# A feed-forward weight kept by halves: one quarter goes out to DRAM and back, one is converted in the double block

## The chip, the cores and the metric

One core of one Trainium2 chip runs the kernel. The metric is the device time of one execution in microseconds (us); several runs are given as their median. Engines are TensorE (PE; its weight loads are PEld), VectorE (DVE), ScalarE (ACT), GpSimd (POOL) and SyncE (SP), whose queue issues nearly all transfers.

## The reference

Three layers follow each other, in float32; the inputs w_in and w_out arrive as 8-byte floats, which the kernel reads as pairs of int32 and converts itself.

```python
def reference(**kwargs):
    attn_out = _attn_ref(**attn_kwargs)      # 4 x 8 heads, 576 positions, 64 columns; causal, with a decay from cumsum(s)
    x = np.ascontiguousarray(attn_out.transpose(0, 2, 1, 3)).reshape(B * S, H * D)   # 2304 x 512
    x = _moe_ref(x=x, **moe_kwargs)          # soft mixture: d.T @ x gives 32 slots, 8 experts of 4 slots, c @ slot_out
    return _moe2_ref(x=x, **moe2_kwargs)     # h = x @ w_in; g = piecewise square of h; g @ w_out
```

In the mixture, slot_out has 32 rows of 512, c is 2304 x 32, and x = c @ slot_out. So h = x @ w_in = c @ (slot_out @ w_in): the product M = slot_out @ w_in, 32 x 2048, is made once, and the hidden products have only 32 rows to sum over (96 with the parts of a split float).

## The kernel before, in words

**Attention** (lines 166 to 672). 32 heads go in 16 pairs. A plan of times (PLAN, GATE, one pair is 12 units; `at` and `step` put an action at a time) is sorted and gives each engine's order. Among its actions are `next(pre)` from `load_parts` (line 116), which issues one load of an expert weight tile (128 x 1024 floats, 512 KB) into a free slot, and the steps W0 to W4, which advance `convert_wi` (line 606): a chunk of w_in is loaded (128 x 512 int32), GpSimd scales the high words (L626), VectorE shifts the low words (L627) and joins them (L629) into `wif`, which holds all of w_in, four quarters, unfinished. `finish_wi` (line 633) ends the conversion by four VectorE operations for each of 16 parts (L639 to L642); they run in the experts' stage.

**Experts** (lines 713 to 832). `layer1` and `layer2` take the eight experts in turn; W_ORDER is the order of the 64 weight tiles. 22 slots (16 named post, N_LEFT = 6 named pre) are filled in attention; when attention's memory is freed, 6 more pre slots (N_RIGHT) and 10 others (N_TMP) follow. `release` gives a layer's slots back and `load_w` issues the next loads, in one order on SP's queue. Tiles of w_out (wo) follow the experts' on that queue, six at a time at most, all but the first two behind a small `gate` transfer that waits for the last expert tile.

**Double block** (from line 834). A step is one (j, c): 384 tokens and 128 of the 2048 hidden columns; the first two blocks of tokens go side by side, so 16 columns take 32 steps. A step i of the loop at line 954 does: VectorE's g and ScalarE's gh of step i - 1 (`g_part`, L889, L891); TensorE's hidden product hp of step i and ScalarE's two w (`h_part`, L879, L881, L882); a part of the conversion of w_out, in five parts per tile (`convert_wo`: ScalarE's Prelu cv, VectorE's shift and join, ScalarE's cast wh, VectorE's rest wl; L154 to L158, L786, L788), one tile in two steps; VectorE's gl of step i - 1 (`l_part`, L897); and the nine output products of step i - 2 (`o_part`, L907 to L909).

hp reads 96 rows of `mst`: M twice rounded, and its rest. Before the loop, `m_part` makes the first 128 columns of all four quarters (16 products), `split_m` writes the first quarter's into mst (ScalarE twice, VectorE once; L858, L859), then come the other 384 columns (16 products), `split_m` again, and `stack_m` (L863 to L868), which rounds the other three quarters in m_hi and m_lo and carries their rows into mst by nine transfers.

The program adds semaphore waits itself. For two engines that touch one bank of PSUM it lets one wait for the other; each transfer waits for the one eight before it (eight counters, DMAHW0 to DMAHW7, in turn).

## Time and profile before

| | |
|---|---|
| runs, median of 3 | 460.08 us (459.59 to 461.58) |
| profiled execution, own time | 463.19 us |
| its span | 461.4 us |
| PE, DVE, ACT, POOL busy | 443.8, 326.7, 339.0, 45.3 us |
| moved by transfers | 71.02 MB |
| mean granted TensorE clock | 0.98 |

A busy time is the sum of an engine's instructions. TensorE counts as busy in 96% of the span whether or not its products come as closely as they could, so the table does not say what bounds a stage; the chain of waits and the starts of single instructions do. All times in the sections below are from the start of the span of the profiled execution.

### The profile page before, as it was taken

What the parts mean: (1) busy time and instruction counts of PE and PEld (TensorE: products, weight loads), DVE (VectorE), ACT (ScalarE), POOL (GpSimd) and SP (SyncE); (2) the same over time, 40 slices, a digit from 0 to 9 for tenths busy, and PEclk for the clock granted to TensorE, in tenths of its full rate; (3) what the DMA queues carried; (4) which work ended last, traced back from release to release, by engine and by line L of the source; (5) the groups of instructions that cost most, each with busy time, mean ns of one, the idle gap of its engine ahead of it and who ended that gap; (6) DMA issues with size and microseconds to landing.
All of it is one profiled execution on the core that took longest, in us unless ns stands there. A gap on an engine that the chain in (4) does not pass through costs nothing.

```text
span 461.4 us, 11656 instructions
## 1 busy us (share of the span) xinstructions
PE 443.8 (96%) x4306; PEld 336.8 (73%) x4306; DVE 326.7 (71%) x966; ACT 339.0 (73%) x914; POOL 45.3 (10%) x168
## 2 busy tenths in 40 slices
PE   7999999999999998898889999999999999999996
PEld 2676766776777676566546888888888888888885
DVE  6687899899988863699838888866555555455543
ACT  6998998998999894122248999977677767777673
POOL 2222212422222111000000000000000000000000
PEclk9799999999999998799999999999999999999999
DMA  3888879977897258699985900003001001001001
GB/s 86 228 219 217 255 218 294 265 225 192 221 279 237 67 170 287 216 390 407 409 294 196 362 2 1 0 2 136 1 0 68 1 1 70 1 0 56 14 1 68
DMA packets 28554, 71.02 MB, mean 154 GB/s; under 512 B 4018, under 2 KB 5490, under 8 KB 28498
## 3 DMA queue, kind: packets, MB, share of 16 engines
q1 hardware_dynamic: 28342, 70.14, 47.7%
q8 instruction: 34, 0.56, 0.5%
q14 instruction: 22, 0.18, 0.2%
q10 hardware_dynamic: 156, 0.14, 0.1%
HBM read 64.83 MB, written 4.83 MB: 151 GB/s over the span
## 4 chain that ended last, share of the span: by engine, by line
PE 83%; DVE 6%; DMA 5%; ACT 4%; issue 2%; POOL 0%; ACTq 0%; POOLq 0%; DVEq 0%; SPq 0%
PE o L909 14%; PE o L907 14%; PE o L908 14%; PE s L291 9%; PE s L399 7%; PE s L360 5%; DMA wt<-in_w_dram 4%; PE hp L879 4%; PE s L434 3%; PE p L736 2%; PE s L299 2%; PE s L391 2%; PE p L752 2%; ACT P L350 1%; DVE s L305 1%
## 5 line engine op out<-in xcount | busy, mean ns | idle before, releaser
L907 PE MATMUL o<-wt,gh 128*128 128x512 f32 x288 | 112.6, 391 | 0.6 <-ACT gh L891 0.6
L909 PE MATMUL o<-wt,gl 128*128 128x512 f32 x288 | 112.3, 390 | 0.2 <-DVE gl L897 0.2
L908 PE MATMUL o<-wt,gh 128*128 128x512 f32 x288 | 112.1, 389 | 0.0
L350 ACT ACTIVATE P<-s,nm 128x256 f32<-128x256 f32 (+4 forms) x160 | 85.0, 551 | 9.1 <-DVE nm L305 6.8
L897 DVE TENSOR_TENSOR gl<-g,gh 128x384 fp32r<-128x384 f32 x96 | 53.5, 557 | 42.1 <-ACT gh L891 42.0
L305 DVE CUSTOM_DVE_ANT_0 s<-s,tri 128x256 f32<-128x256 f32 (+4 forms) x160 | 74.0, 506 | 12.6 <-PE s L291 6.2
L891 ACT CAST gh<-g 128x384 fp32r<-128x384 f32 x96 | 49.3, 513 | 45.1 <-DVE g L889 42.6
L889 DVE SCALAR_TENSOR_TENSOR g<-w,hp 128x384 f32<-128x384 f32 x96 | 53.1, 553 | 37.2 <-ACT w L882 37.2
L907 PEld LDWEIGHTS o<-wt,gh 128*128 128x128 f32 x288 | 54.3, 188 | 12.8 <-ACT gh L891 1.1
L909 PEld LDWEIGHTS o<-wt,gl 128*128 128x128 f32 x288 | 54.0, 188 | 12.5 <-DVE gl L897 1.3
L908 PEld LDWEIGHTS o<-wt,gh 128*128 128x128 f32 x288 | 54.4, 189 | 7.5
L291 PE MATMUL s<-x 64*128 64x512 f32 (+3 forms) x256 | 57.1, 471 | 0.0
L881 ACT ACTIVATE w<-hp,half 128x384 f32<-128x384 f32 x96 | 55.4, 577 | 0.8 <-PE hp L879 0.8
L882 ACT ACTIVATE w<-w 128x384 f32<-128x384 f32 x96 | 50.4, 525 | 3.0
L383 ACT COPY pts<-s 128x512 f32<-128x512 f32 (+3 forms) x128 | 47.8, 463 | 1.5 <-PE s L360 0.5
L360 PEld LDWEIGHTS s<-ident,P 64*128 64x128 f32 x800 | 38.6, 142 | 10.9 <-ACT P L350 4.8
L360 PE MATMUL s<-ident,P 64*128 64x64 f32 x800 | 44.2, 229 | 2.3 <-ACT P L350 2.2
L399 PE MATMUL s<-pts,v 128*64 128x512 f32 (+3 forms) x256 | 38.9, 446 | 0.0
L350 ACT ACTIVATION_READ_ACCUMULATOR P<-s,nm 128x1 f32 x160 | 36.8, 230 | 0.0
L879 PE MATMUL hp<-cstack,mst 96*128 96x384 f32 x96 | 32.6, 343 | 0.3 <-DVE mst L859 0.3
L291 PEld LDWEIGHTS s<-x 64*128 64x128 f32 x256 | 29.3, 196 | 4.2 <-DMA x<-in_qkT_dram 1.5
L399 PEld LDWEIGHTS s<-pts,v 128*64 128x64 f32 x256 | 18.5, 141 | 17.5 <-issue 15.3
(149 smaller groups left out, 567.2 us busy)
## 6 DMA issues: line engine op xcount, KB each, us to landing
wt<-in_w_dram SPq DMA_DIRECT2D x64, 512.0 KB
x<-in_qkT_dram SPq DMA_DIRECT2D x32, 288.0 KB
st<-in_w_in_dram SPq DMA_DIRECT2D x32, 256.0 KB
wt<-in_w_out_dram SPq DMA_DIRECT2D x16, 512.0 KB
out_dram<-ob SPq DMA_DIRECT2D x17, 256.0 KB
v<-in_v_main_dram SPq DMA_DIRECT2D x16, 256.0 KB
ext<-exts SPq DMA_DIRECT2D x60, 3.4 KB
v<-in_v_tail_dram SPq DMA_DIRECT2D x16, 32.0 KB
```

Of the source, the lines that this page charges most:

```text
L291: T.matmul(out=o[h][:, off:off + n], lhsT=y[r, 0, c:c + 128], rhs=y[r, 1, 0:n], start=(k == 0), stop=(k == 1))
L305: V.tensor_tensor_reduce(out=sc, in0=sc, in1=mask[:, mask.shape[1] - n:], scale=-1.0 / SCALE, scalar=init, op0=ALU.add, op1=ALU.min, accum ...
L350: A.activation(out=out_, in_=in_, func=AF.Exp, bias=nm, scale=-1.0, accum_out=sm[:, k:k + 1])
L360: T.transpose(out=o[f][:, c:c + 64], in_=P[r], identity=ident[r, r])
L399: T.matmul(out=o[r, 128 * j:512], lhsT=vt[:, j, r], rhs=pts_t[pi][:, h, 512 * j:384 * j + 512], start=(j == 0), stop=(j == 3))
L879: T.matmul(out=hp, lhsT=mst[0:96, 128 * c:128 * c + 128], rhs=cstack[0:96, BLK * j:BLK * j + BLK], start=True, stop=True)
L881: A.activation(out=w, in_=hp, func=AF.Relu, bias=half, scale=0.5)
L889: V.scalar_tensor_tensor(out=g, in0=w, scalar=1.0, in1=hp, op0=ALU.min, op1=ALU.max)
L897: V.tensor_tensor(out=gl, in0=g, in1=gh.bitcast(F32), op=ALU.subtract)
L907: T.matmul(out=o_t[j][t], lhsT=gh[:, r], rhs=wh[c], start=(c == 0), stop=False)
L908: T.matmul(out=o_t[j][t], lhsT=gh[:, r], rhs=wl[c], start=False, stop=False)
L909: T.matmul(out=o_t[j][t], lhsT=gl[:, r], rhs=wh[c], start=False, stop=(c == 15))
```

## The change

w_in is no longer kept whole. `wif` has room for two quarters (WI_KEEP = 2), which takes 16 KB less on each partition, and N_LEFT goes from 6 to 10 slots of 4 KB. In attention, three quarters are converted. Quarter 2 (WI_AWAY) comes first: it is finished at once, by a third VectorE operation per chunk, and each chunk is stored to DRAM (w_in_f) by a transfer on SP's queue. Quarters 0 and 1 follow as before; `finish_wi` has 8 parts. The conversion's steps move to the pairs of W_PAIRS, and four early loads are added at four times near attention's end (PRE_AT).

Quarter 3 (WI_LATE) is loaded raw after the experts, by `load_wi`, called ahead of M: four tiles of it, then two of quarter 2 back from DRAM, all into pre slots. The loop converts quarter 3 by `convert` (the Prelu, shift and join of w_out) at the steps 5, 7, 8, 10, 11, 13, 14 and 16. M is made by quarters: 0 and 1 before the loop, 2 and 3 by 16 products each behind hp of the steps 10 and 18, in the 128 columns of the bank that hp leaves free. `split_m` writes quarter 0 in four parts, and `stack_m` carries a quarter's rows by 12 transfers of 32 x 128.

```diff
@@ -30,8 +30,12 @@
...
 N_HOME = 16
-N_LEFT = 6
+N_LEFT = 10
 N_RIGHT = 6
+WI_KEEP = 2
+WI_AWAY = (2,)
+WI_LATE = (3,)
+W_PAIRS = (1, 2, 3, 4, 6, 7, 8, 10, 11, 12, 14)
 N_TMP = (7, 3)
...
@@ -48,13 +52,15 @@
...
 CHUNK = 256
-WI_0 = (0,)
+WI_0 = (0, 3)
 WARM_T = (9, 4, 2, 3, 4)
-PRE_FROM, PRE_STEP = (5, 2.4)
+PRE_AT = [3 * int(5 + 2.4 * _n) + 0.76 for _n in range(22)] + [171.76, 177.76, 183.76, 186.76]
 NWIN = 2
...
 BLK = 384
+M_AT = {10: 2, 18: 3}
+LATE_AT = 5
...
@@ -101,10 +107,12 @@
...
-    wif = wip.tile([128, 4, 4, 512], F32, name="wif")
+    wif = wip.tile([128, WI_KEEP, 4, 512], F32, name="wif")
+    w_dram = ctx.enter_context(tc.tile_pool(name="w_dram", bufs=1, space=bass.MemoryType.DRAM))
+    w_in_f = {fb: w_dram.tile([128, 2048], F32, name=f"w_in_f{fb}") for fb in WI_AWAY}
     w_src = {"w1": w1, "w2": w2, "wo": w_out.bitcast(I32)}
-    w_tiles, w_wo, wo_used = {}, {}, []
+    w_tiles, w_wo, w_wi, wo_used = {}, {}, {}, []
     w_next = [0]
...
@@ -600,39 +608,57 @@
...
         pre = load_parts()
-        for n in range(N_HOME + N_LEFT):
-            at(3 * int(PRE_FROM + PRE_STEP * n) + 0.76, lambda: next(pre, None))
+        for t in PRE_AT:
+            at(t, lambda: next(pre, None))
+
+        n_fb = 2048 // CHUNK
+        wi_order = [(fb, k) for fb in (*WI_AWAY, *range(WI_KEEP)) for k in range(n_fb)]
...
-            n_all = 2048 * 4 // CHUNK
-            sts = {}
+            sts, spill = {}, []
             def get(n):
-                if n < n_all:
-                    fb, k = divmod(n, 2048 // CHUNK)
+                if n < len(wi_order):
+                    fb, k = wi_order[n]
                     sts[n] = stage.tile([128, 2 * CHUNK], I32, tag="st", name="st")
                     nc.sync.dma_start(out=sts[n], in_=w_in.bitcast(I32)[fb, :, 2 * CHUNK * k:2 * CHUNK * (k + 1)])
+
+            def put():
+                if spill:
+                    fb, k, d = spill.pop(0)
+                    nc.sync.dma_start(out=w_in_f[fb][:, CHUNK * k:CHUNK * (k + 1)], in_=d)
...
             yield
-            for n in range(n_all):
-                fb, k = divmod(n, 2048 // CHUNK)
+            for n, (fb, k) in enumerate(wi_order):
                 st = sts.pop(n)
-                d = wif[:, fb].rearrange("p c f -> p (c f)")[:, CHUNK * k:CHUNK * (k + 1)]
+                away = fb in WI_AWAY
+                d = wif[:, WI_KEEP - 1 if away else fb].rearrange("p c f -> p (c f)")[:, CHUNK * k:CHUNK * (k + 1)]
+                di = d.bitcast(I32)
                 w = st.rearrange("p (n two) -> p n two", two=2)
...
                 G.tensor_scalar(d, hi.bitcast(F32), 2.0 ** -112, 1.0, op0=ALU.mult, op1=ALU.mult)
-                V.tensor_scalar(lo, lo, 1, 0x70000000, op0=ALU.logical_shift_right, op1=ALU.bitwise_and)
+                if away:
+                    V.tensor_scalar(lo, lo, 29, None, op0=ALU.logical_shift_right)
+                    yield
+                    V.scalar_tensor_tensor(out=di, in0=di, scalar=3, in1=lo, op0=ALU.logical_shift_left, op1=ALU.bitwise_or)
+                    yield
+                    V.scalar_tensor_tensor(out=di, in0=hi, scalar=-0x80000000, in1=di, op0=ALU.bitwise_and, op1=ALU.bitwise_or)
+                else:
+                    V.tensor_scalar(lo, lo, 1, 0x70000000, op0=ALU.logical_shift_right, op1=ALU.bitwise_and)
+                    yield
+                    V.tensor_tensor(out=di, in0=di, in1=lo, op=ALU.bitwise_or)
+                get(n + 2)
+                put()
+                if away:
+                    spill.append((fb, k, d))
                 yield
-                V.tensor_tensor(out=d.bitcast(I32), in0=d.bitcast(I32), in1=lo, op=ALU.bitwise_or)
-                get(n + 2)
-                yield
...
-            for n in range(16):
+            for n in range(4 * WI_KEEP):
                 fb, k = divmod(n, 4)
...
@@ -660,7 +686,7 @@
...
                     step(n, f, pi)
-            for k in range(5) if pi else WI_0:
+            for k in (range(5) if pi in W_PAIRS else ()) if pi else WI_0:
                 step(f"W{k}", next, cw, None)
...
@@ -840,47 +866,81 @@
...
-    M_A = 128
-    mp = [ps_e.tile([128, 512], F32, tag="e", name="mp") for _ in range(2)]
-
-    def m_part(a, b, cs):
-        for c in cs:
-            for fb in range(4):
-                T.matmul(out=mp[a > 0][32 * fb:32 * fb + 32, a:b], lhsT=soT[:, c], rhs=wif[:, fb, c, a:b],
+    mp = [ps_e.tile([128, 128], F32, tag="e", name="mp") for _ in range(WI_KEEP)]
+    ps_w = []
+
+    def m_part(out, w):
+
+        for c in range(4):
+            for g in range(4):
+                T.matmul(out=out[32 * g:32 * g + 32, :], lhsT=soT[:, c], rhs=w(c)[:, 128 * g:128 * g + 128],
                          start=(c == 0), stop=(c == 3))
-    m_hi = fin[0].tile([128, 512], F32R, tag="m_hi", name="m_hi", bufs=1)
-    m_lo = fin[0].tile([128, 512], F32R, tag="m_lo", name="m_lo", bufs=1)
-    ps_w = []
-
-    def split_m(a, b):
+    def split_m(m, g):
+
+        q, c = slice(32 * g, 32 * g + 32), slice(128 * g, 128 * g + 128)
         for r in range(2):
-            A.copy(out=mst[32 * r:32 * r + 32, a:b], in_=mp[a > 0][0:32, a:b])
-        V.tensor_tensor(out=mst[64:96, a:b], in0=mp[a > 0][0:32, a:b], in1=mst[0:32, a:b].bitcast(F32), op=ALU.subtract)
-
-    def stack_m():
-        for r in (slice(0, M_A), slice(M_A, 512)):
-            A.copy(out=m_hi[:, r], in_=mp[r.start > 0][:, r])
-            V.tensor_tensor(out=m_lo[:, r], in0=mp[r.start > 0][:, r], in1=m_hi[:, r].bitcast(F32), op=ALU.subtract)
-        for fb in range(1, 4):
+            A.copy(out=mst[32 * r:32 * r + 32, c], in_=m[q])
+        V.tensor_tensor(out=mst[64:96, c], in0=m[q], in1=mst[0:32, c].bitcast(F32), op=ALU.subtract)
+
+    def stack_m(fb, m):
+
+        m_hi, m_lo = (fin[0].tile([128, 128], F32R, tag=n, name=n, bufs=2) for n in ("m_hi", "m_lo"))
+        A.copy(out=m_hi, in_=m)
+        V.tensor_tensor(out=m_lo, in0=m, in1=m_hi.bitcast(F32), op=ALU.subtract)
+        for g in range(4):
             for r in range(3):
-                nc.sync.dma_start(out=mst[32 * r:32 * r + 32, 512 * fb:512 * fb + 512].bitcast(F32),
-                                  in_=(m_hi if r < 2 else m_lo)[32 * fb:32 * fb + 32].bitcast(F32))
-        ps_e_ctx.close()
-        ps_w.append(ctx.enter_context(tc.tile_pool(name="ps_w", bufs=2, space=PSUM)))
-
+                nc.sync.dma_start(out=mst[32 * r:32 * r + 32, 512 * fb + 128 * g:512 * fb + 128 * g + 128].bitcast(F32),
+                                  in_=(m_hi if r < 2 else m_lo)[32 * g:32 * g + 32].bitcast(F32))
+
+    def slot_tile(dtype=F32):
+
+        slot = next(f for f in w_free if f[0] == "pre")
+        w_free.remove(slot)
+        t = slot[1].tile([128, 1024], F32, tag="w", name="wi")
+        return (t if dtype == F32 else t.bitcast(dtype)), slot
+
+    def load_wi():
+
+        for fb in WI_LATE:
+            for c in range(4):
+                raw, slot = slot_tile(I32)
+                nc.sync.dma_start(out=raw, in_=w_in.bitcast(I32)[fb, :, 1024 * c:1024 * c + 1024])
+                if c % 2 == 0:
+                    t = slot_tile()[0]
+                out_ = t[:, 512 * (c % 2):512 * (c % 2) + 512]
+                w_wi[fb, c] = out_
+                late.append((convert(raw, out_, out_), slot))
+        for fb in WI_AWAY:
+            for n in range(2):
+                t = slot_tile()[0]
+                nc.sync.dma_start(out=t, in_=w_in_f[fb][:, 1024 * n:1024 * n + 1024])
+                w_wi[fb, 2 * n], w_wi[fb, 2 * n + 1] = t[:, 0:512], t[:, 512:1024]
+
+    late = []
+
+    def kept(fb):
+        return lambda c: wif[:, fb, c]
+
+    def back(fb):
+        return lambda c: w_wi[fb, c]
...
-    def h_part(j, c):
-        hp = ps_h.tile([128, BLK], F32, tag="h", name="hp")
+    def h_part(j, c, fb=None):
+        hm = ps_h.tile([128, 512], F32, tag="h", name="hp")
+        hp = hm[:, 0:BLK]
         T.matmul(out=hp, lhsT=mst[0:96, 128 * c:128 * c + 128], rhs=cstack[0:96, BLK * j:BLK * j + BLK], start=True, stop=True)
+        if fb is not None:
+            m_part(hm[:, BLK:512], back(fb))
         w = ew.tile([128, BLK], F32, tag="w", name="w")
...
         g_t[j, c] = hp, w
+        if fb is not None:
+            return lambda: stack_m(fb, hm[:, BLK:512])
...
@@ -932,16 +992,17 @@
...
+    load_wi()
     one_c = gens[WO_EARLY]
     next(one_c)
-    m_part(0, M_A, range(4))
-    split_m(0, M_A)
+    m_part(mp[0], kept(0))
+    split_m(mp[0], 0)
     next(one_c)
     next(one_c)
-    m_part(M_A, 512, range(1))
     h_part(*seq[0])
     h_part(*seq[1])
-    m_part(M_A, 512, range(1, 4))
+    for fb in range(1, WI_KEEP):
+        m_part(mp[fb], kept(fb))
     g_part(*seq[0])
...
@@ -949,18 +1010,32 @@
...
     o_next()
-    split_m(M_A, 512)
-    stack_m()
+    for g in range(1, 4):
+        split_m(mp[0], g)
+    for fb in range(1, WI_KEEP):
+        stack_m(fb, mp[fb])
+    ps_e_ctx.close()
+    ps_w.append(ctx.enter_context(tc.tile_pool(name="ps_w", bufs=2, space=PSUM)))
+    late_at = {}
+    for n in range(len(late)):
+        for f in range(2):
+            late_at.setdefault(LATE_AT + 3 * n + 2 * f, []).append((n, 2 - f))
     for i in range(1, len(seq) + 1):
+        stack = None
         if 2 < i:
...
         if 1 < i < len(seq):
-            h_part(*seq[i])
+            stack = h_part(*seq[i], M_AT.get(i))
         for n in conv.get(i, []):
             next(gens[n], None)
+        for n, k in late_at.get(i, []):
+            for _ in range(k):
+                next(late[n][0])
         if 2 < i:
...
             o_next()
+        if stack:
+            stack()
     while done[1] < len(seq):
...
```

What a program's order shows at three places (line numbers of the kernel before are those of the profile; the changed kernel has its own).

First, SP's queue from the end of attention to the first rows of M; wt are weight tiles, wi quarters of w_in, mst the rows of M. Before:

```order
L140 DMA wt<-in_w_dram 128x1024 x38
L140 DMA wt<-in_w_out_dram 128x1024
L140 DMA wt<-in_w_dram 128x1024 x4
L140 DMA wt<-in_w_out_dram 128x1024
L133 DMA gate<-wt 1x1
L140 DMA wt<-in_w_out_dram 128x1024 x6
L867 DMA mst<-m_hi 32x512 x2
L867 DMA mst<-m_lo 32x512
L867 DMA mst<-m_hi 32x512 x2
```

With the change:

```order
L148 DMA wt<-in_w_dram 128x1024 x36
L148 DMA wt<-in_w_out_dram 128x1024
L148 DMA wt<-in_w_dram 128x1024 x4
L148 DMA wt<-in_w_out_dram 128x1024
L141 DMA gate<-wt 1x1
L148 DMA wt<-in_w_out_dram 128x1024 x5
L908 DMA wi<-in_w_in_dram 128x1024 x4
L917 DMA wi<-w_in_f_147 128x1024 x2
L148 DMA wt<-in_w_out_dram 128x1024
L893 DMA mst<-m_hi 32x128 x2
L893 DMA mst<-m_lo 32x128
L893 DMA mst<-m_hi 32x128 x2
```

Two early loads are among the 36. Behind the gate stand six tiles of w_in, ahead of M's rows, and the first quarter's rows are twelve transfers (four such threes) where three were.

Second, ScalarE between the first gh and the third w; mp is M in PSUM, mst its rows, cv the Prelu of w_out. Before:

```order
L891 CAST gh<-g 128x384 [waits DVE_49] x2
L858 CAST mst<-mp 32x384 [waits PE_49]
L858 CAST mst<-mp 32x384
L863 CAST m_hi<-mp 128x128
L863 CAST m_hi<-mp 128x384 [waits DVE_49]
L154 ACTIVATE cv<-wt 128x512 [waits DMAHW6_49]
L881 ACTIVATE w<-hp,half 128x384 [waits PE_49]
```

With the change:

```order
L951 CAST gh<-g 128x384 [waits DVE_49] x2
L883 CAST mst<-mp 32x128 x2
L883 CAST mst<-mp 32x128 [waits DVE_49]
L883 CAST mst<-mp 32x128
L883 CAST mst<-mp 32x128 [waits DVE_49]
L883 CAST mst<-mp 32x128
L889 CAST m_hi<-mp 128x128 [waits PE_49]
L162 ACTIVATE cv<-wt 128x512 [waits DMAHW6_49]
L939 ACTIVATE w<-hp,half 128x384 [waits PE_49]
```

Two casts of 384 columns became six of 128; the third and the fifth of them wait for VectorE, whose subtraction (L884) of the pair before them reads the same bank. One m_hi of 128 columns is left.

Third, VectorE around step 10 of the loop (g and gl of the steps 9 and 10; wt and cv belong to w_out, wi to quarter 3). Before:

```order
L889 SCALAR_TENSOR_TENSOR g<-w,hp 128x384 [waits Activation_49]
L788 TENSOR_TENSOR wt<-cv,wt 128x512 [waits Activation_49]
L158 SCALAR_TENSOR_TENSOR cv<-cv,wt 128x512 [waits DVE_49]
L897 TENSOR_TENSOR gl<-g,gh 128x384 [waits PE_49,Activation_49]
L889 SCALAR_TENSOR_TENSOR g<-w,hp 128x384 [waits Activation_49]
```

With the change:

```order
L949 SCALAR_TENSOR_TENSOR g<-w,hp 128x384 [waits Activation_49]
L814 TENSOR_TENSOR wt<-cv,wt 128x512 [waits Activation_49]
L166 SCALAR_TENSOR_TENSOR cv<-cv,wt 128x512 [waits DVE_49]
L166 SCALAR_TENSOR_TENSOR wi<-wi 128x512
L957 TENSOR_TENSOR gl<-g,gh 128x384 [waits PE_49,Activation_49]
L890 TENSOR_TENSOR m_lo<-hp,m_hi 128x128 [waits PE_49,Activation_49]
L949 SCALAR_TENSOR_TENSOR g<-w,hp 128x384
L164 TENSOR_SCALAR wt<-wt 128x512 [waits DMAHW1_49]
L164 TENSOR_SCALAR wi<-wi 128x512 [waits DMAHW5_49]
```

A join of wi stands ahead of gl of step 9, and m_lo between it and g of step 10; g has no wait of its own any more, since m_lo's for ScalarE (m_hi, which stands behind cv there) is the later one.

## Rows read from the trace of the kernel before

**Rows 1.** Chain of waits, attention, value products of pairs (start us, us, what)
```profile
62.49 2.16 PE s L399 x16
...
74.87 2.16 PE s L399 x16
...
94.07 2.16 PE s L399 x16
...
116.84 2.15 PE s L399 x16
```

**Rows 2.** Chain of waits, the experts
```profile
205.44 1.86 PE p L736 x32
...
209.53 1.86 PE p L736 x32
...
225.62 10.15 DMA wt<-in_w_dram
```

**Rows 3.** Windows (stretch, length, busy and count by engine, PEclk, DMA share, GB/s)
```profile
155.00:160.00 5.00, 5.00 (x73) 3.25 (x71) 4.71 (x23) 4.17 (x13) 1.07 (x5) 1.00 0.01 3
...
190.00:195.00 5.00, 4.53 (x51) 3.17 (x51) 3.53 (x9) 0.69 (x2) 0.00 (x0) 0.84 0.24 59
...
225.00:230.00 5.00, 3.69 (x85) 2.40 (x85) 3.82 (x7) 0.39 (x1) 0.00 (x0) 1.00 1.03 408
```

**Rows 4.** Timeline (start, us, instruction), VectorE and TensorE in the double block
```profile
255.61 0.55 DVE L897 TENSOR_TENSOR gl<-g,gh 128x384 fp32r<-128x384 f32 x1
...
255.80 0.34 PE L879 MATMUL hp<-cstack,mst 96*128 96x384 f32 x1
...
256.43 0.39 PE L909 MATMUL o<-wt,gl 128*128 128x512 f32 x1
...
258.02 0.34 PE L879 MATMUL hp<-cstack,mst 96*128 96x384 f32 x1
```

**Rows 5.** Timeline, ScalarE and VectorE in the double block, one turn of the loop
```profile
270.76 0.53 ACT L882 ACTIVATE w<-w 128x384 f32<-128x384 f32 x1
...
271.19 0.60 ACT L786 CAST wt<-cv 128x512 fp32r<-128x512 f32 x1
...
271.32 0.55 DVE L889 SCALAR_TENSOR_TENSOR g<-w,hp 128x384 f32<-128x384 f32 x1 [0.48 <-ACT w L882]
...
271.91 0.52 ACT L891 CAST gh<-g 128x384 fp32r<-128x384 f32 x1
...
273.04 0.55 DVE L897 TENSOR_TENSOR gl<-g,gh 128x384 fp32r<-128x384 f32 x1
...
273.51 0.55 DVE L889 SCALAR_TENSOR_TENSOR g<-w,hp 128x384 f32<-128x384 f32 x1
```

**Rows 6.** Instructions of the tile wif (count, ns least/median/most, first and last start)
```profile
L642 DVE TENSOR_TENSOR wif<-wif,cw x16: 691/693/693, 194.5 to 228.3; 128x512 int32<-128x512 int32 x16
```

**Rows 7.** Timeline, ScalarE and VectorE ahead of the loop
```profile
238.77 0.52 ACT L858 CAST mst<-mp 32x128 fp32r<-32x128 f32 x2 [0.75 <-PE mp L849]
...
239.33 0.28 DVE L859 TENSOR_TENSOR mst<-mp,mst 32x128 fp32r<-32x128 f32 x1 [5.51 <-ACT mst L858]
...
243.35 0.95 ACT L858 CAST mst<-mp 32x384 fp32r<-32x384 f32 x2
...
244.66 0.55 DVE L859 TENSOR_TENSOR mst<-mp,mst 32x384 fp32r<-32x384 f32 x1
...
245.25 0.48 ACT L863 CAST m_hi<-mp 128x384 fp32r<-128x384 f32 x1 [0.66 <-DVE mst L859]
...
245.62 0.67 ACT L154 ACTIVATE cv<-wt 128x512 f32<-128x512 f32 x1
```

**Rows 8.** Timeline, TensorE, the first products of M
```profile
237.60 1.08 PE L849 MATMUL mp<-wif,soT 128*32 128x128 f32 x32
```

**Rows 9.** Timeline, SP's queue, M's rows, the first and the last of nine
```profile
245.75 1.21 SPq L867 DMA_DIRECT2D mst<-m_hi  x2
...
251.84 0.59 SPq L867 DMA_DIRECT2D mst<-m_lo  x1
```

## The prediction

> **What bounds the kernel now.** I read the chain of waits first, then the table of windows, then the timelines of the stages that the diff touches. The kernel has three stages, and each has another limit.
>
> Attention (to about 193 us) is bound by TensorE: in the chain, one pair of heads follows the other by its value products. Two pairs without gate work take 94.07 - 74.87 = 19.2 us, so 9.6 each; the pair with the first gate takes 74.87 - 62.49 = 12.38, and the next gate pair together with its neighbour 116.84 - 94.07 = 22.77, that is 13.17 beyond a plain pair [rows 1].
>
> The experts (193 to 237 us) are bound by the transfers of w1 and w2. The reader sees it in the chain: TensorE takes 209.53 - 205.44 = 4.09 us per expert as long as the tiles are there, and then it waits for tiles: the last one takes 10.15 us from issue to landing, at 235.8 [rows 2]. The windows show when the transfers run: 408 GB/s from 225 to 230 us, but 3 GB/s from 155 to 160 and 59 from 190 to 195, where every slot is full [rows 3].
>
> The double block (from 237 us) is bound by TensorE again: its hidden products stand 258.02 - 255.80 = 2.22 us apart [rows 4]. But the elementwise loop beside it is nearly as long. ScalarE's w, VectorE's g (waits for w), ScalarE's gh (waits for g) follow each other without a gap, and g to g is 273.51 - 271.32 = 2.19 us [rows 5]. So the loop gains only some 0.04 us per step on TensorE.
>
> **The change, part by part.**
>
> *Four more slots.* The queue's order shows 42 expert tiles before and 40 now after the last v load, two of which are early loads: 38 tiles are left for the experts' stage, 4 fewer. A tile has 524,288 bytes; at 408 GB/s that is 1.285 us, so 4 are 5.1 us. The four go where the transfers idle [rows 3], so I cost them at nothing; if that cover were gone, they would cost the 5.1 again. Is something late next? TensorE at 4.09 per expert from 209.53 would start the last first layer at 221.8 and end the last second layer at about 227.7; the last tile landed at 235.8 [rows 2], now 230.7. The transfers still bind: **-5.1**. VectorE's finishing of w_in ran to 229.0 in 16 rounds of (228.3 - 194.5) / 15 = 2.25 us [rows 6]; without halving it would have held M up at 229; 8 rounds end near 211.
>
> *Attention.* Chunks go from 32 to 24, the away ones with one VectorE operation more each, five operations per pair as before, and none in the pairs 5, 9 and 13, which hold the gates. The second gate pair costs 13.17 against 12.38 for the first: 0.8 more, of which 0.2 is its rescaling and neighbour. I take back half of what may be VectorE's, 0.3 in each of two pairs: **-0.6**; bounds -1.2 (all of it) and +0.5, since eight stores enter SP's queue and pair 14 gets five operations that it did not have.
>
> *Before the first products.* mp of the first quarter is one bank, and the order now shows ScalarE's second and third pair of casts each waiting for VectorE. Before, two casts took 0.95 us from 243.35, VectorE was free at 244.66, the second m_hi waited 0.66 for it, and cv began at 245.62 [rows 7]. Now: casts of 32x128 are 0.52 a pair and the subtraction 0.28 [rows 7]. First pair 243.35 to 243.87; VectorE 244.66 to 244.94; second pair to 245.5; VectorE to 245.8; third pair to 246.4; m_hi, and cv at 246.6. That is **+1.0**, on the path, because the loop that starts here is what TensorE waits for.
> The wait of 0.66 has ScalarE and VectorE on the same 32 rows of a bank, so it does not tell whether other rows need one. [...]
>
> *M in the stream.* 16 products of 128 columns took 1.08 us with the tail of the last [rows 8]; between others I take 0.85. Two quarters: **+1.7** on TensorE, the engine that binds. What they leave in the prologue is worth nothing, since there gh was waited for.
>
> *The conversions in the loop.* Per added operation I ask how much later the next g or gh comes. ScalarE's conversion lies beside VectorE's g: from w, 0.43 to the conversion and its 0.60 make 1.03, and gh starts 1.15 after w (270.76, 271.19, 271.91) [rows 5]. An added Prelu takes 0.67 alone [rows 7], some 0.1 less where the next follows at once, so it pushes gh by 0.4. Four of them, at steps 5, 8, 11 and 14: 1.6. At steps 10 and 18 g must now follow m_lo, and m_lo follows m_hi, which stands behind cv: g starts 0.43 + 0.57 + 0.26 + 0.28 = 1.54 after w (the last two by the cast and the subtraction of [rows 7]) and not 0.56, 1.0 each, 2.0 in all. In even steps VectorE is just in time (gl ends, g starts: 273.04, 273.51 [rows 5]); the last conversion's 0.6 at step 16 pushes g by 0.6. Loop: 4.2 us later. Against it stand 0.85 at each of steps 10 and 18, in which TensorE itself is busy with M, 0.04 per step, and the margin at the start: gl of step 5 ends at 256.16, its product starts at 256.43, so 0.27 [rows 4]. Walking it step by step (extra work between g and gl, 0.4 to 0.6 at steps 8, 10, 14 and 16, comes off the margin as well) TensorE stalls 0.1 at step 5, 0.3 at 8, 0.4 at 11, 0.3 at 14 and 0.55 at 16: **+1.6**. Bounds: 0 (all hidden) and 4.2 (nothing hidden).
>
> *M's rows* cost nothing by the sum: those of quarter 1 are issued from about 241 and needed twelve us later; that they are late is a rival.
>
> Sum: -5.1 - 0.6 + 1.0 + 1.7 + 1.6 = **-1.4 us**. The profiled execution took 463.19, so 461.8 by its own time; the median of the three runs is 460.08, 3.1 below it, and I set the difference against the median: **458.7**.
>
> **The rivals.**
>
> *The loop's extra work hides.* For it: ScalarE is not busy all through a step. Against it: what is idle lies between operations that wait for each other [rows 5]. Then the sum lacks the 1.6, 457.1; and if the casts do not alternate either, another 1.4, 455.7. It would be 0.5% faster or more.
>
> *M's rows come late: slower.* Place: SP's queue after the gate, where the rows of quarter 1 now stand behind twelve tiles and not eight, and are 12 transfers where 3 were. Nine took 245.75 to 252.43 to issue [rows 9], 0.74 each, so 12 take 8.9; from 241.3 (cv at 246.6, m_lo just after it, less 5.7) the last is issued at 250.2. In the full queue a transfer took 10.15 to land [rows 2], so 260.4; step 8 [rows 4] needs them at 258.02 - 5.7 + 1.0 + 0.4, about 253.7. That is 6.7 us late, 465.4. It decides if the twelve are waited for together; the code reads 128 columns at a time, so three are enough for steps 8 and 9, and these land, even at 10.15 each, at 253.7. [...]
>
> *Nothing hides in the loop.* All 4.2 stall, and attention gives nothing: -5.1 + 1.0 + 1.7 + 4.2 = +1.8, 461.9. The walk speaks against it: M's own time covers most of steps 10 and 18.
>
> *The four tiles do not get earlier.* SP's queue works in order; if the last early loads stood behind waiting ones, the experts would end as before, +3.7, 463.8. Against it: they are issued before the tiles whose slots are still in use.
>
> **How the numbers follow.** A measurement here tells some 0.5%, 2.3 us, from no change. Forecast 0.53, within 457.2 to 460.2; the hidden loop 0.28; nothing hidden 0.08; late rows 0.07; tiles not earlier 0.04. Faster takes the second case and the part of the forecast that attention pushes under 457.8: 0.34. Slower takes the last two and a little of the third: 0.12. The rest, 0.54, is the same. The range leaves out the last two cases and the extreme ends of the second: 455.8 to 461.5.
>
> **What would show it.** Right: M's first product about 5 to 6 us earlier (near 232); the next cv 9 us after it and not 8 (245.62 - 237.60); hidden products more than 2.22 apart at steps 5 to 20, some 3 us in all, and 2.22 after. Wrong: TensorE waiting for mst from a transfer; the experts' transfers with a pause after 195; pairs of heads over 9.6 us early in attention.

## The result: slower by 0.7%, and the profile after

| | before | change |
|---|---|---|
| median of 13 runs | 459.04 us (458.36 to 461.58) | 463.62 us (460.63 to 465.72) |
| profiled execution, own time / span | 463.19 / 461.4 us | 465.64 / 463.8 us |
| mean granted TensorE clock in it | 0.980 | 0.987 |

The medians stand 4.6 us apart. The ratio is 1.0073, with a 95% interval of 1.0052 to 1.0094: 2.4 to 4.3 us slower, where 1.4 us faster was forecast. The time lies outside the range, on the other side.

One pair of traces does not show where this comes from, since their first 200 us differ by more than the change does. So both kernels were profiled once more (e1 and e2 below), and a table of stages is read from all four. Each stage ends at a row that the program has in both versions: the first and the last value products (L399 before, L407 now), the first expert's first product, the issue of `gate` (which waits for the last expert tile), M's first product, and the hidden products (hp) of steps 4, 20, 37 and 95.

| stage, us | before | e1, before again | change | e2, change again | e2 - e1 |
|---|---|---|---|---|---|
| start to first value products | 22.00 | 21.75 | 23.74 | 20.82 | -0.93 |
| to the last value products | 154.67 | 153.10 | 152.28 | 152.05 | -1.05 |
| to the first expert | 16.46 | 13.49 | 16.01 | 13.51 | 0.02 |
| to the last tile (gate) | 42.66 | 42.24 | 37.65 | 37.71 | -4.53 |
| to M's first product | 1.81 | 1.81 | 3.84 | 3.14 | 1.33 |
| to hp of step 4 | 10.37 | 10.37 | 11.30 | 11.29 | 0.92 |
| to hp of step 20 | 36.69 | 36.71 | 40.50 | 40.51 | 3.80 |
| to hp of step 37 | 37.74 | 37.74 | 38.91 | 39.58 | 1.84 |
| to hp of step 95 | 128.76 | 128.76 | 128.77 | 128.76 | 0.00 |
| to the end of the span | 10.23 | 10.22 | 10.84 | 10.78 | 0.56 |
| span | 461.39 | 456.19 | 463.84 | 458.15 | 1.96 |

The first stage (but for one instruction of VectorE's) and the third hold the same instructions in both kernels, and they move by up to 3 us from one trace of a kernel to the next. Attention moved by 1.6 between the two of before (single pairs of 10.2 to 10.6 us, at other places in e1 than in the first), the tiles by 0.4, and two stages in which the change waits for something new by 0.7; the others repeat within 0.1. Without the first and third, e2 is 2.9 us slower than e1, within what the runs measured.

**Attention** is as forecast. The chain has the same pairs as [rows 1]; the plain ones are 9.6 us apart (84.49 - 74.90), and the stretch with the second gate takes 116.44 - 94.08 = 22.36 where it took 22.77. Columns are start, length, what.

```profile
62.56 2.16 PE s L407 x16
...
74.90 2.16 PE s L407 x16
...
84.49 2.15 PE s L407 x16
...
94.08 2.16 PE s L407 x16
...
116.44 2.16 PE s L407 x16
```

**The experts.** The tiles come 4.5 to 5.0 us sooner, as the sum has it. But TensorE is no longer waiting for them. `gate` is issued at 229.68, so the last tile is there; TensorE's last batch of products begins only at 231.74. SP's queue and TensorE in the timeline of the change:

```profile
229.68 0.68 SPq L141 DMA_DIRECT2D gate<-wt  x1
```

TensorE:

```profile
227.97 0.64 PE L778 MATMUL p<-wt,hT 128*32 128x128 f32 x16
228.55 0.55 PE L756 MATMUL idle<-ident 128*128 128x128 f32 x3
229.03 0.64 PE L778 MATMUL p<-wt,hT 128*32 128x128 f32 x15
230.01 0.27 PE L778 MATMUL p<-wt,hT 128*32 128x128 f32 x1 [0.35 <-issue]
230.21 0.55 PE L756 MATMUL idle<-ident 128*128 128x128 f32 x3
230.69 0.64 PE L778 MATMUL p<-wt,hT 128*32 128x128 f32 x16
231.26 0.55 PE L756 MATMUL idle<-ident 128*128 128x128 f32 x3
231.74 0.64 PE L778 MATMUL p<-wt,hT 128*32 128x128 f32 x16
...
233.52 1.08 PE L876 MATMUL mp<-wif,soT 128*32 128x128 f32 x32
```

Between the batches stand nine idle transposes (L756). Before, they ran while TensorE waited for tiles; [rows 2] has that wait in the chain up to 235.8. Now they stand in the way, and M's first product comes 3.84 us after the last tile and not 1.81.

**Ahead of the loop** ScalarE shows the alternation that was forecast: it waits 0.99 and 0.35 us for VectorE between pairs of casts. cv starts 242.49 - 233.52 = 8.97 us after M's first product, where [rows 7, 8] give 8.02.

```profile
239.36 0.53 ACT L883 CAST mst<-mp 32x128 fp32r<-32x128 f32 x2
240.88 0.53 ACT L883 CAST mst<-mp 32x128 fp32r<-32x128 f32 x2 [0.99 <-DVE mst L884]
241.77 0.53 ACT L883 CAST mst<-mp 32x128 fp32r<-32x128 f32 x2 [0.35 <-DVE mst L884]
242.32 0.27 ACT L889 CAST m_hi<-mp 128x128 fp32r<-128x128 f32 x1
242.49 0.66 ACT L162 ACTIVATE cv<-wt 128x512 f32<-128x512 f32 x1
```

**The loop** is late around steps 10 and 18. These are TensorE's hp rows of steps 9, 10 and 11, with M's products behind that of step 10:

```profile
257.18 0.34 PE L935 MATMUL hp<-cstack,mst 96*128 96x384 f32 x1
...
259.81 0.34 PE L935 MATMUL hp<-cstack,mst 96*128 96x384 f32 x1
260.08 1.08 PE L876 MATMUL hp<-wi,soT 128*32 128x128 f32 x32
...
263.27 0.34 PE L935 MATMUL hp<-cstack,mst 96*128 96x384 f32 x1
```

Step 10 takes 2.63 and step 11 3.46, that is 0.41 and 1.24 over the 2.22 of [rows 4]. At step 18 it is 0.58, at 19 1.25, at 16 0.21. Steps 5 and 6 are as late as before (0.64 and 0.54), and up to step 35 no other is late by over 0.05. TensorE never waits for a transfer into mst (the six waits of hp and its weight load, 4.1 us, all end with VectorE): M's rows come in time.

**Two late steps that no term foresaw.** The double block writes the first two blocks of tokens, six tiles, about step 34, through four output buffers (ob). The fifth of the six copies, ScalarE's, waits 0.93 us for the first output transfer to land, and the sixth, VectorE's, 1.49 us for the second. The next g stands behind that sixth copy. The chain of waits of the change, with the second transfer:

```profile
315.90 0.35 SPq L982
...
316.35 3.72 DMA out_dram<-ob
...
320.15 0.69 DVE ob L155
320.85 0.47 DVE g L949
...
321.90 0.50 PE o L967
```

Steps 36 and 37 are 0.51 and 0.65 late. In e2 this transfer takes 4.42. In both traces of before no copy waits over 0.05 us for these transfers, and hp stays at 2.22.

### The profile page after: what moved, and what is told of

It reads as the page before. It is cut to its first block, busy times and chain, and to the rows that moved or that the text cites. A ratio compares the mean times of both kernels' runs of the same rounds, so it can differ in the third digit from the quotient of the medians.

```text
span 463.8 us, 11795 instructions
## 1 busy us (share of the span) xinstructions
PE 446.6 (96%) x4370; PEld 338.5 (73%) x4370; DVE 312.2 (67%) x937; ACT 340.9 (73%) x923; POOL 42.0 (9%) x160
## 4 chain that ended last, share of the span: by engine, by line
PE 74%; ACT 11%; DVE 6%; DMA 5%; issue 2%; SPq 1%; POOL 0%; ACTq 0%; DVEq 0%; POOLq 0%
PE s L299 9%; PE o L967 9%; PE o L969 9%; PE o L968 9%; PE s L407 7%; PE s L368 6%; PE s L442 4%; PE p L762 4%; PE p L778 3%; DVE g L949 3%; PE s L307 3%; PE s L399 3%; ACT gh L951 3%; ACT w L940 2%; ACT w L939 2%; PE hp L935 2%
## 5 line engine op out<-in xcount | busy, mean ns | idle before, releaser
L368 PE MATMUL s<-ident,P 64*128 64x64 f32 x800 | 43.1, 230 | 2.1 <-ACT P L358 1.9
L358 ACT ACTIVATION_READ_ACCUMULATOR P<-s,nm 128x1 f32 x160 | 37.8, 236 | 0.0
L407 PE MATMUL s<-pts,v 128*64 128x512 f32 (+3 forms) x256 | 37.3, 433 | 0.0
L407 PEld LDWEIGHTS s<-pts,v 128*64 128x64 f32 x256 | 17.2, 137 | 17.0 <-issue 14.6
```

Source lines behind the costliest of these rows:

```text
L358: A.activation(out=out_, in_=in_, func=AF.Exp, bias=nm, scale=-1.0, accum_out=sm[:, k:k + 1])
L368: T.transpose(out=o[f][:, c:c + 64], in_=P[r], identity=ident[r, r])
L407: T.matmul(out=o[r, 128 * j:512], lhsT=vt[:, j, r], rhs=pts_t[pi][:, h, 512 * j:384 * j + 512], start=(j == 0), stop=(j == 3))
```

## The experiments

The kernels are variants of the changed one unless it is said. Times are medians, ratios are to the kernel before on the same chip. Where a stage is the question, it is read from the experiment's trace, because medians move with the first and third stage.

**e1, e2: both kernels again.** No edit.

> The kernel before, unchanged, for a second trace. Theory: the start is uneven from run to run (first ScalarE exponential at 10.6 us in the first trace of before, 12.4 us in that of the change, with the same program up to there), and two early pairs of heads took 10.6 and 10.25 us in place of 9.6 by chance, so this trace shows a start between 10 and 13 us, early pairs at 9.6, and an execution near 459 to 461 in place of 463.2. Rival: the slow early pairs are the program's own (conversion beside the pair) and stand again at 10.6 and 10.25, with an execution near 463.

> The changed kernel, unchanged, for a second trace and for times on the same chip as the others. Theory (collision with program code): the fifth copy of the first output blocks waits again some 1.2 us for the first output transfer, because a 16,384-byte load of program code falls on it at the same instruction; hidden products near 321 us stand 2.7 and 2.9 apart again. Rival (chance): that wait is gone in this trace and the time 1 us less. Both expect the stalls at steps 10, 11, 18 and 19 (some 3.7 us over 2.22 a step, M's products included) to stand again to 0.2 us.

e1 took 457.99, its early pairs 9.6 apart: those of 10.6 and 10.25 in the first trace were chance (e1 has one of 10.33 later). e2's profiled run took 459.94, its six runs 459.94 to 465.40 (ratio 1.0097, 1.0062 to 1.0132). The stalls at steps 10, 11, 18 and 19 stand again (0.50, 1.25, 0.57, 1.25), and so do the two late steps after the output (1.21 and 0.63). They are the program's.

What the first output transfers meet is in the list of DMA queues. From 309 to 316 us in e2:

```profile
GB/s 0 0 0 0 0 0 0 0 246 456 351 374 351 374 386 363 340 374 374 304 35 12 12 35 304 386 374 386 71 35 23 23 23 23 23 23 328 421 386 328
...
q1 hardware_dynamic: 705, 1.30, 50.0%
q8 instruction: 1, 0.02, 1.5%
```

One 16,384-byte load of program code (queue q8) falls into the transfers. By its packet's record it starts at 310.70 and keeps one of the 16 DMA engines for 1.62 us (1.5% of 16 engines in 7 us); 15 of the first transfer's 16 parts signal their end by 311.26, the last at 313.35. The rates of 35, 12, 12 and 35 GB/s, 23.5 in the mean, fit that one engine, alone at work: a sixteenth of the 374 before them is 23.4. The second transfer, issued 0.44 us after the first, has one late part too: 15 of its 16 counts on the semaphore stand by 312.30, the last at 314.47. In e1 the loads come at 295.74 and 324.76, and the same stretch of its list has q1 alone:

```profile
q1 hardware_dynamic: 864, 1.57, 60.2%
```

So a load of 1.62 us goes with one part of 16 late by 2.1 us (313.35 - 311.26). The first trace of the change has the same: a load from 316.99, 1.18 us long, 15 parts of the first output transfer by 317.94 and the last at 319.43, 1.49 later. In the first trace of before, with no load there, the 16 parts end within 0.15 us (317.04 to 317.19).

**e3: no idle transposes in the last expert.**

```diff
-WARM_E = (4, 3, 2, 4)
+WARM_E = (4, 0, 2, 4)
```

> The nine idle transposes between the batches of the last expert's second layer left out; the output does not depend on them. Theory (TensorE is late at the experts' end, not the tiles): the last tile landed at 229.7 us in the change's trace but TensorE ended its batch on it at 232.3; nine transposes take 1.45 us of that, so M's first product comes 1.2 to 1.5 us earlier and so does the end. Rival (the wait for hT or for tiles sets it): under 0.3 us. Rival (clock): without idle work the granted clock falls after 230 and the time is 1 us or more longer.

462.95 us on e2's chip, where the change had 464.47 (ratios 1.0078 and 1.0097, whose intervals overlap, so the stage decides). M's first product comes 2.26 us after gate, so 0.9 sooner than in e2 and 1.6 sooner than in the first trace; what is left of the 1.2 to 1.5 the tile itself now holds (gate at 227.54, the last batches from 227.61). The rival of the clock is out: after 193 us it does not fall before the span's last microseconds (1.00 in the windows from 194 to 206, PEclk 9 in each later slice of the page). TensorE's timeline in e3:

```profile
227.61 1.07 PE L778 MATMUL p<-wt,hT 128*32 128x128 f32 x30 [0.76 <-issue]
...
229.80 1.08 PE L876 MATMUL mp<-wif,soT 128*32 128x128 f32 x32
```

**e4: casts first.**

```diff
-        for r in range(2):
-            A.copy(out=mst[32 * r:32 * r + 32, c], in_=m[q])
-        V.tensor_tensor(out=mst[64:96, c], ...)
+        for q, c in qc:
+            for r in range(2):
+                A.copy(out=mst[32 * r:32 * r + 32, c], in_=m[q])
+        for q, c in qc:
+            V.tensor_tensor(out=mst[64:96, c], ...)
...
-    for g in range(1, 4):
-        split_m(mp[0], g)
+    split_m(mp[0], (1, 2, 3))
```

> The six casts of the first quarter's parts 1 to 3 are written ahead of their three subtractions, where they alternated. Theory (alternation costs 1.0 us): ScalarE no longer waits 0.99 and 0.35 between pairs of casts; m_hi and cv start 1.2 to 1.3 us earlier (cv 7.7 us after M's first product in place of 9.0), the loop starts 1.0 to 1.3 earlier, and so does the end. Rival (VectorE takes it over): three subtractions and m_lo, 1.15 us, now follow the casts and the loop's first g waits for them; under 0.4 us.

The six casts run in one piece and cv starts 7.65 us after M's first product (8.96 in e2): 1.3 less. VectorE's subtractions cost it a part: to hp of step 4 the stage takes 10.38, 0.9 less, as long as before. 463.09 us on e2's chip. ScalarE's timeline in e4:

```profile
236.87 1.62 ACT L884 CAST mst<-mp 32x128 fp32r<-32x128 f32 x6
238.51 0.27 ACT L891 CAST m_hi<-mp 128x128 fp32r<-128x128 f32 x1
238.67 0.66 ACT L162 ACTIVATE cv<-wt 128x512 f32<-128x512 f32 x1
```

**e5: m_hi and m_lo behind the next g.**

```diff
         if 2 < i:
             g_part(*seq[i - 1])
+        if held:
+            held.pop()()
...
-            stack()
+            held.append(stack)
```

> The split of M's quarters 2 and 3 into m_hi and m_lo is issued one step later, behind that step's g and gh, so that g of steps 10 and 18 no longer follows m_lo on VectorE. Theory (the stack's place costs it): from the hidden product of step 4 to that of step 20 the traces of the change take 40.5 us, 5.0 over 16 steps of 2.22 less the 1.2 that before has too, so 3.8; M's own products are 1.7 of it, and g's wait for m_lo is the rest, so this falls to 38.4 to 39.2. Rival (the conversions of quarter 3 use up the margin): it stays above 40.0. The wait at the first output transfer stays in both.

The theory falls. g of step 10 now runs ahead of m_lo (260.31 and 261.60 in VectorE's timeline), and TensorE's steps 10, 11, 18 and 19 are 0.51, 1.23, 0.49 and 1.24 late, as before the edit. The median is 463.15 us (ratio 1.0066, 1.0037 to 1.0095). (In e5 and e6 TensorE's granted clock is at half from 235 to 242, so the stages there are not compared.)

**e6: quarter 3 not converted.**

```diff
         for n, k in late_at.get(i, []):
-            for _ in range(k):
-                next(late[n][0])
+            pass
...
+                w_wi[fb, c] = wif[:, 1, c]
```

The raw tiles are still loaded, and M's quarter 3 is made from quarter 1's weights.

> Leaves out the conversion of w_in's quarter 3 in the loop (eight times a Prelu or two integer operations); its raw tiles are still loaded, and M's quarter 3 is made from quarter 1's weights, so its values are not the reference's. Theory of the prediction (the conversions stall TensorE by 1.6 us, 0.1 to 0.55 at steps 5, 8, 11, 14 and 16): from the hidden product of step 4 to that of step 20 it takes 38.9 us in place of 40.5. Rival (the margin takes the conversions; m_lo ahead of g at steps 10 and 18 makes the stalls): above 40.0, and only the 0.2 at step 16 is gone.

Neither size was right. Steps 11 and 19 stay 1.24 late each, and steps 10, 16 and 18 are on time. From step 7 to 20 the excess falls from 3.83 (e2) to 2.50: the conversions cost 1.3, at steps 10, 16 and 18, and M's products cost 1.24 a quarter, 2.5 in all. 462.24 us. TensorE's hp in e6, steps 9 to 11, with M's products:

```profile
254.83 0.34 PE L931 MATMUL hp<-cstack,mst 96*128 96x384 f32 x1
...
257.05 0.34 PE L931 MATMUL hp<-cstack,mst 96*128 96x384 f32 x1
257.33 1.08 PE L876 MATMUL hp<-wi,soT 128*32 128x128 f32 x32
258.34 0.50 PE L963 MATMUL o<-wt,gh 128*128 128x512 f32 x1
...
260.51 0.34 PE L931 MATMUL hp<-cstack,mst 96*128 96x384 f32 x1
```

M's 16 products hold TensorE for 258.34 - 257.33 = 1.01 us. The other 0.2 stands at their two ends: the first begins 0.28 after hp, where a product of w_out begins 0.18 after it, and the second product behind them (258.68) 0.34 after the first, where 0.23 is usual.

What the conversions delay is in e2's timeline, between hp of step 9 (250.81) and step 10 (253.53):

```profile
249.65 0.69 DVE L814 TENSOR_TENSOR wt<-cv,wt 128x512 fp32r<-128x512 f32 x1
...
250.25 0.69 DVE L166 SCALAR_TENSOR_TENSOR cv<-cv,wt 128x512 int32<-128x512 int32 x1
...
250.86 0.42 DVE L164 TENSOR_SCALAR wi<-wi 128x512 int32<-128x512 int32 x1
...
251.19 0.55 DVE L957 TENSOR_TENSOR gl<-g,gh 128x384 fp32r<-128x384 f32 x1
...
251.80 0.50 PE L969 MATMUL o<-wt,gl 128*128 128x512 f32 x1 [0.20 <-DVE gl L957]
```

At step 8 VectorE runs two operations of w_out's conversion and then one of quarter 3's ahead of gl, and TensorE's product that reads this gl waits 0.20 for it. The products around the wait begin 0.59 and 0.33 apart and not 0.23, so a wait of 0.20 makes step 10 0.50 late. At step 16 it is the same, with a wait of 0.26 and step 18 late by 0.57. At step 14 gl ends at 266.53 and its product begins at 266.58, 0.27 and 0.34 from its neighbours, so step 16 is 0.18 late. In e6 TensorE has no such wait.

**e7: TensorE's code shifted.**

```diff
-N_IDLE = 7
+N_IDLE = 3
...
+        for _ in range(34):
+            T.matmul(out=idle[:, 0:64], lhsT=ext[1][:, 0, 0:128], rhs=ext[1][:, 0, 0:64], ...)
```

> At the start, where TensorE waits for its first rows, four of the seven idle products of 512 columns are replaced by 34 of 64 columns: 30 instruction pairs more, of no consequence for the output. Theory (a load of TensorE's code holds up the first output transfer): the 16,384-byte loads come every 256 TensorE instructions, some 28.4 us apart in the loop; 60 instructions earlier is 6.7 us earlier, so the load falls near 304 and not on the first six output transfers; the two late steps after them (2.7 to 3.4 and 2.9 in place of 2.22) are gone, and the time is 1.2 to 1.8 us less. Rival (chance, or too few output buffers at the new pace): the late steps stay and the time is the same.

The load falls at 301.58 (near 304 was expected), eight us ahead of the first output transfer. From 309 to 316 the list has q1 alone, and hp is 2.22 apart from step 20 on (37.74 from step 20 to 37). 460.70 us, ratio 1.0013 (0.9981 to 1.0045): the change's 0.7% is gone but for what its interval leaves open. The two late steps are 1.2 to 1.8 us of that; the rest is within the intervals. Its runs still spread from 457.43 to 463.67. The list of DMA queues from 309 to 316, and hp in the same stretch, in e7:

```profile
q1 hardware_dynamic: 864, 1.57, 60.2%
```

TensorE's timeline:

```profile
310.31 0.34 PE L937 MATMUL hp<-cstack,mst 96*128 96x384 f32 x1
...
312.54 0.34 PE L937 MATMUL hp<-cstack,mst 96*128 96x384 f32 x1
...
314.75 0.34 PE L937 MATMUL hp<-cstack,mst 96*128 96x384 f32 x1
```

**e8, e9: seven more idle transposes at attention's end**, in the change (e8) and in the kernel before (e9).

```diff
-WARM_T = (9, 4, 2, 3, 4)
+WARM_T = (9, 8, 5, 3, 4)
```

> At the end of attention seven more idle transposes of TensorE, four where it waits 0.52 us for mx and three where it waits 0.43 us for nm; they change nothing in the output. In three of four traces of the change the granted clock falls to half for 6.8 to 10.2 us between 173 and 196, and the first expert then starts 16.0 to 16.5 us after the last pair's value products; in the trace without it 13.5. Theory (TensorE's pauses there let the clock fall, and this is what spreads the times of the change from 460 to 465): this trace shows 13.5 and a clock of 1.0 there, and the times gather within 459.5 to 461.5. Rival (the clock falls whatever is put there): 16.0 or more in the trace, times from 460 to 465 as before.

> The kernel before with the same seven idle transposes at the end of attention as in e8_warm. Theory (the fall of the clock there takes time from both kernels, more often from the change): its times gather within 457.2 to 458.8, the first expert starts 13.5 us after the last value products, and e8_warm (458.5) is then 0.3 to 1.2 us slower than this, in place of the 3.4 to 4.5 between the two without it. Rival (only the change suffers): the median stays at 459 to 460 and e8_warm is faster than before with the same transposes.

Windows of the change's first trace show where the times part: TensorE's granted clock is at half (0.50) while it makes the gate's last products, after pauses of 0.46, 0.52, 0.43 and 0.41 us since the last value products, and the first expert starts 16.01 us after these. In e8 the clock is full (1.00) and it is 13.52. Columns as in [rows 3], PEclk the third from the end; first the change:

```profile
185.00:188.00 3.00, 3.00 (x29) 0.80 (x27) 1.76 (x7) 0.00 (x0) 0.47 (x1) 0.54 0.85 344
188.00:191.00 3.00, 3.00 (x15) 2.50 (x14) 1.33 (x4) 0.69 (x2) 0.00 (x0) 0.50 0.00 0
191.00:194.00 3.00, 2.52 (x23) 1.55 (x26) 2.30 (x5) 0.00 (x0) 0.00 (x0) 0.50 0.43 94
```

The same place in e8:

```profile
182.00:185.00 3.00, 2.87 (x38) 1.56 (x36) 2.42 (x10) 0.34 (x1) 0.47 (x1) 1.00 0.90 365
185.00:188.00 3.00, 2.52 (x33) 1.96 (x34) 2.10 (x7) 0.69 (x2) 0.00 (x0) 1.00 0.21 48
188.00:191.00 3.00, 2.46 (x46) 1.26 (x41) 2.86 (x6) 0.76 (x2) 0.00 (x0) 1.00 0.95 264
```

Of the seven traces of the change and its variants without the transposes (change, e2 to e7) five show the clock at half somewhere between 173 and 196 us; of the five with them (e8 to e12) none does.

e8 took 458.52 us (ratio 0.9975, 0.9954 to 0.9996), and 11 of its 12 runs lie between 457.50 and 460.05. Its 14 more instructions also moved the code load, to 306.25, and the two late steps are gone, so against e2 it shows two things at once. Against e7, which has the code moved and not the clock held, it is 2.2 us less (458.52, 460.70), though the two intervals overlap. e9 took 458.86 (ratio 0.9982, 0.9963 to 1.0001), so the gain in the kernel before is not clear of noise, and e8 is not 0.3 to 1.2 us slower than e9, as was expected, but as fast. With the clock held and the code load out of the way, the change and the kernel before stand within 0.4 us of each other.

**e10: the four early tiles undone**, in e8.

```diff
-    w_free = list(wpre)
+    w_free = list(wpre[:-4])
...
-    w_free += slots(tmp_ctx, "tmp", N_TMP[1])
+    w_free += slots(tmp_ctx, "tmp", N_TMP[1]) + wpre[-4:]
```

> e8_warm with its last four weight slots given out only when the experts' stage begins, so 22 tiles are loaded ahead as in before; all else as in e8_warm. Theory (four tiles are 5.1 us of transfers, but TensorE ends 1.3 us after the tiles): from the first expert's start to the last tile 42.2 to 42.8 us in place of 37.7, M's first product 1.8 us after the last tile in place of 3.0, so M's products and the end 3.3 to 4.0 us later. Rival (the four hide anyway): under 1 us. Rival (nothing but the tiles counts): 5.0.

463.41 us, where e8 took 458.52. First expert to last tile takes 43.03 (37.66 in e8), M's first product follows 1.80 after it (2.97), and the two stages together are 4.2 longer: 5.4 of transfers, 1.2 of it given back by TensorE. That is a little over the 3.3 to 4.0 that were expected.

**e11, e12: together.** e11 is e8 with e3, e4 and

```diff
-        late_at.setdefault(LATE_AT + 3 * n + 2 * f, []).append((n, 2 - f))
+        late_at.setdefault(LATE_AT + 2 * n + 2 * f, []).append((n, 2 - f))
```

> e8_warm with e3_no_idle and e4_casts_first, and the conversions of quarter 3 put on the steps 5, 7, 9, 11 and 13 (they stood on 5, 7, 8, 10, 11, 13, 14 and 16), where the conversion of w_out gives VectorE one short operation and not two long ones. Theory (the terms add): M's first product 0.9 earlier against the last tile, cv 1.2 to 1.3 earlier against M's first product, and of the 1.25 at steps 10, 16 and 18 some 0.8 to 1.2 gone: 3.0 us under e8_warm, so 455 to 456. Rival (the steps with two long operations are not the cause; ScalarE's two Prelus in one step are not either): the stalls move to other steps and it is 2.1 under e8_warm.

457.59 us, ratio 0.9938 (0.9921 to 0.9955), where 455 to 456 was expected. M's first product stands 1.81 after the last tile, cv 7.62 after it, and steps 9, 13 and 16 are 0.22, 0.19 and 0.15 late where 10, 16 and 18 were 1.3: half of the conversions' cost is gone and half moved to other steps. But without the nine transposes the code load fell on the output transfers again (309.56), and two steps are 0.84 and 0.66 late. e12 adds e7's edit.

> e11_combined with the 30 more instruction pairs at the start as in e7_code_shift. In e11_combined the load of TensorE's code fell on the first output transfers again (at 309.6, two us after the first issue) and two steps were 0.84 and 0.66 late. Theory: the load falls 5 to 8 us earlier, those 1.5 us are gone, and the median is 455.8 to 456.4, with hidden products all 2.22 apart from step 20 on. Rival (something else makes these two steps late): 457.4 or more.

456.53 us, ratio 0.9931 (0.9909 to 0.9953), the lowest median here and faster than both kernels; from e11 the ratios do not tell it apart. The load is at 299.17 and step 20 to 37 takes 37.74, 1.5 less than in e11 (39.24).

## Why the prediction was wrong

Term by term, with e2 - e1 and the experiments:

| term | forecast | measured |
|---|---|---|
| four tiles fewer to wait for | -5.1 | -4.5 to -5.0, -5.2 (e8 - e9), 5.4 (e10) |
| TensorE after the last tile | 0 | +1.2 to +2.0 |
| attention | -0.6 | -0.9 (e8 - e9), -1.05 (e2 - e1) |
| before the first products | +1.0 | +0.9 |
| M in the stream | +1.7 | +2.5 |
| the conversions and m_lo in the loop | +1.6 | +1.3 |
| code load on the output transfers | not in the sum | +1.2 to +1.8 |
| end of the span | not in the sum | +0.55 |

**The step that failed first** is "Is something late next?". Taking TensorE at its pace, it has the last second layer end at "about 227.7" and concludes "The transfers still bind". The first trace has it end at 232.4, 2.7 us after the last tile. The pace of 4.09 per expert holds only inside the row of experts. The last one also has its own chain (hs, transposes, hT) and nine idle transposes in its second layer, which the trace of before hides in waits for tiles. Of the 5 us that the slots give, TensorE hands back 1.2 to 2.0. e3 takes most of that back (2.26 from the last tile to M's first product), e11 all of it (1.81).

**The largest miss is not in any step**: the new wait at the first output transfers, 1.2 to 1.8, and the end. The sum ended at step 20, because nothing in the diff touches what comes after; but the places at which TensorE's code is loaded moved with the instructions of its stream: from 310.70 (e2) to 301.58 with e7's 60 more and to 306.25 with e8's 14 more. e7 and e12 show the first: moving the load away, with nothing changed around those steps, gives the 2.22 back. The end is only argued: in e2 an 8,192-byte load of code (queue q14) stands at 455.90, among the last output transfers, and in e1 at 457.33, after the span. It is so in every trace: with this load inside the span the end takes 10.71 to 10.92 (the change and its variants), with it after the span 10.22 or 10.23 (before, e1, e9). No run moved it.

**M** was mis-sized: 0.85 a quarter was chosen under the 1.08 of [rows 8], to leave out the tail of the last. The 16 take 1.01 between others, the products at their ends 0.2 more, and hp to hp is 1.24 longer (e6).

**The conversions** cost 1.3 where 1.6 was forecast; that the size is near is in part luck, for the mechanism is another. Steps 5, 8, 11 and 14 were to be late mostly by ScalarE's Prelu, and at steps 10 and 18 g was to be late behind m_lo. What is late is VectorE's gl, behind the parts of quarter 3 at steps 8, 14 and 16, and TensorE's steps 10, 16 and 18 with it; the part at step 10 hides under M's products. The prediction has this work between g and gl only as something that comes off a margin. e5 shows m_lo to cost nothing (M's own 1.24 covers it), and e11 halves the cost by moving the eight parts to steps in which VectorE has one operation of w_out's conversion and not two.

**Right** were the tiles, the alternation of the casts (0.99 and 0.35 of wait, cv 8.97 after M's first product for "9 us"), attention's sign and size, M's rows in time, and so the price given to that rival. The alternation is the program's own wait for a bank: e4 removes it by order alone, and cv then starts 7.65 us after M's first product, near the 7.6 (245.2 - 237.60) of an estimate without these waits from [rows 7, 8]: three pairs of casts of 0.52 from 243.35 on and one m_hi of half a pair, 0.26.

**Of the rivals** none happened as told. "Nothing hides in the loop" comes nearest in time (461.9) and for a wrong reason; the mechanism named for the slower side, M's rows, did not act. In the account of that rival, six tiles of w_out stood behind the gate before, by the queue's order, and not eight; its 6.7 us stay the same. No run shows the 1.4 us that "The loop's extra work hides" takes off for casts that do not alternate; with the casts in one piece, e4 has cv 1.3 sooner and the stage to hp of step 4 0.9 shorter than e2.

**Medians.** The stages tell 2.9 us, of 3.4 by the ratio and 4.6 between the medians. The rest fits the clock at attention's end, though no run shows it alone: holding it goes with 2.2 us less in the change (e7 to e8) and 0.8 less in the kernel before (its ratio of 0.9982), and both are at the edge of the noise. Why the clock falls there more often in the change, with the same instructions in that stretch, stays open.

## What to carry to other kernels

When a wait for transfers gets shorter, follow the waiting engine's own chain to the end of the stage, with everything that was put into its gaps, before the gain is booked. Read a small change stage by stage in two traces of each kernel; medians mix it with what changes from run to run. Where a late step stands behind a transfer with few buffers, look in the list of DMA queues for a code load in the same microseconds, and move it by some instructions on that engine (14 in e8, from 310.70 to 306.25; 60 in e7, to 301.58).

## What was not expected of the hardware

TensorE's code comes in 16,384-byte loads on queue q8, some 28 us apart in the loop: at 295.74, 324.76, 353.7 and 382.06 in e1. Between two of them, from the first of these four to the end, stand 246 to 263 of TensorE's instructions; in the first trace of before the six loads from 300.94 to 442.85 are 28.4 us and 255.8 instructions apart in the mean, beside the 256 and 28.4 that e7's expectation has. In the loop TensorE has no wait at any of these loads (0 us). A transfer that is spread over all 16 DMA engines was held up by them: 1.2 to 1.8 us in each of the seven traces in which the load met it (the change, e2 to e6, e11), and none in e7, e8, e10 and e12.

TensorE's granted clock fell to half (0.50) in a stretch in which the last pauses of its instructions were 0.41 to 0.52 us (the change's windows above), and did not in another run of the same program, after the same pauses (e2: 0.41 to 0.52, and 1.00 in that stretch). With it the way from the last value products to the first expert is 2.5 us longer (16.01 - 13.51).
